# Attention units staggered: a unit's loads, scores and softmax traced ahead of its predecessor's outputs

## The chip, the cores and the metric

The kernel runs on 1 core of one Trainium2 chip. The metric is the device time of an execution in microseconds (us). "PE" is TensorE (matmuls), "ACT" ScalarE, "DVE" VectorE, "POOL" GpSimd, "SP" the engine that issues nearly all transfers.

## The reference, cut to what matters

```
scores = q @ k^T / sqrt(D)             # q, k, v: (4, 8, 576, 64), float32
scores = where(0 <= i - j < 128, scores - slope[h] * |i - j|, -1e9)
attn   = softmax(scores)
x      = (attn @ v) as (2304, 512)     # tokens x (head, d)
h      = relu(x @ w_in1);  g = s * h * h + b;  y = g @ w_out1
out    = relu(y @ w_in2) ** 2 @ w_out2 # d_model 512, d_ff 2048 in both layers
```

The attention is windowed: a query sees itself and the 127 keys before it. Two feed-forward layers follow. All is float32; the weights come as 64-bit words.

## The kernel before, in words

The 2304 tokens are cut into nine blocks of 256: eight blocks (b, u), batch b and half u of the first 512 positions, and one "tail" block of the last 64 positions of all batches. `blocks` lists them in that order, so block 0 is (0, 0), block 1 (0, 1), block 2 (1, 0), block 3 (1, 1).

Attention of a block is done head pair by head pair, four pairs (HP = 4). `pair_unit` (L190) gives two closures for a pair. `probabilities` (L200) issues the loads of the pair's q, k and v into one buffer `raw`, splits q and k into a high and a low float32r part (`qk`, an ACT copy and a DVE subtraction, L231), makes the scores on PE (L237, tile `s`), adds the bias and takes the row maximum on DVE (L178), exponentiates on ACT (L182) and inverts the denominators on DVE (L185, L186). `outputs` (L247) scales the probabilities (L260 on DVE, L258 on ACT), transposes them on PE (L262, tile `t`, named `tp` in the code), copies them out (ACT, L97), multiplies them with v (L273, tile `u`), and splits the result into the block's inputs `x(b, u)h` (ACT, L94) and `x(b, u)l` (DVE, L100). Units below are written p0 to p3 and o0 to o3: `probabilities` and `outputs` of a block's pairs 0 to 3.

Buffers of the units: `raw` comes from a ring of three (`qkv`), held from the load until the v multiplication; the probabilities come from a ring of four (`pr`), two to a unit, which also holds the rows that go out at the end of a feed-forward block (`result`, tile `xo`); the score banks are two (`s`), `t` and `u` have one bank each, the outputs of a feed-forward block two (`o`), its hidden activations two (`h`).

`mlp` (L326) runs the first layer on a block: for every 128 columns f of d_ff, `first` makes h with twelve matmuls (L348) and squares and splits it (ACT and DVE, L357, L358, L97, L100, tile `g`), and two f later `second_t` adds its product with w_out to the bank (twelve matmuls, L384). The list `behind` holds pieces of other work: before each f some of them are traced, spread evenly. Groups of weights are loaded (`load`, L138, with SP transfers queued behind the last `raw` load traced so far) and turned from 64-bit words to a high and a low part (`conv`, L151, ACT, DVE and POOL, L117 to L122). Weight group g has four f. The parts of groups 0 to 3 are l0/c0 to l3/c3; the last four loads of l3 are staged in the `qkv` ring too.

The sequence at the start: block 0's attention with c0; `half(0)` (block 0 with the first half of d_ff) with l1, c1 and block 1's attention behind it; `half(1)` with block 2's attention (a2) and l2; `half(2)` with c2 and the first two pieces of block 3 (a3); `other(0)` (second half of d_ff) with l3, c3 and the next three pieces of a3; then the rest, four or more pieces to a block. After the first layer the second one runs without attention.

The order of instructions on each engine is not the traced one. A scheduler runs a timeline of the program beforehand and gives each engine, at each moment, the ready instruction that was traced first. The order that comes out is fixed on the chip: an engine waits at its next instruction, whatever stands behind it.

Of the kernel before, what the change touches and what calls it, by code (L numbers as in the profile page):

```python
# [19 lines left out]
def attention_mlp2_kernel(ctx, tc, first0, first1, qkv0, qkv1, qkvt, w_in1, w_out1, s_in, b_in, w_in2, w_out2, out):  # L20
# [8 lines left out]
    B, H = qkv0.shape[:2]  # L29
    NT, DM = out.shape  # L30
    HP = H // 2
# [96 lines left out]
    def group_loads(g, wts, w_in, w_out, staging, steps):  # L128

        f0 = g * GF * P
        parts = [(w, k, n, st) for k, w, st in ((0, w_in, steps[0]), (2, w_out, steps[1])) for n in range(0, GF, st)]
        places = {}

        def load(i):  # L138
            if i == 0:
                wts.append({})  # L140
            w, k, n, step = parts[i]
            rows, n = slice(f0 + n * P, f0 + (n + step) * P), step
            if k == 0:
                w, rows, n = w[:, 2 * rows.start:2 * rows.stop], slice(None), NCC
            src = w[rows].rearrange("(a p) n -> p a n", p=P)
            t = places[i] = staging(i, f"st{g}{i}").rearrange("p a n -> p (a n)").rearrange("p (a n) -> p a n", a=n)

            with tc.issue_after(last_load[0]) if last_load else nullcontext():
                wdma.append(nc.sync.dma_start(t, src).ins)

        def conv(i):  # L151
            _, k, n, step = parts[i]
            if k not in wts[g]:
                for j in (k, k + 1):
                    wts[g][j] = wp.tile([P, GF, DM], F32R, tag=f"{GTAGS[j]}{g}", name=f"{GTAGS[j]}{g}")
            hi, lo = wts[g][k], wts[g][k + 1]
            part = (slice(None), slice(n, n + step)) if k else (slice(None), slice(None), slice(n * P, (n + step) * P))
            convert(places.pop(i).rearrange("p a (n w) -> p a n w", w=2), hi[part], lo[part])
        return [[lambda f=f, i=i: f(i) for i in range(len(parts))] for f in (load, conv)]
# [6 lines left out]
    def new_x(i):  # L166
        xt[i] = [xp.tile([P, NCC, BLK], F32R, tag="x" + y, name=f"x{i}{y}") for y in "hl"]
# [113 lines left out]
    def first_pair(u, hp):  # L281
        for p in pair_unit(0, u, hp):
            p()
# [117 lines left out]
    def finish1(nm, dram):  # L401
        def f(po):
            for t in range(2):
                xo = result(f"xo{nm}{t}")
                act_copy(xo, po[t])
                nc.sync.dma_start(dram[:, 2 * t:2 * t + 2, :].rearrange("p a n -> p (a n)"), xo)
        return f
# [16 lines left out]
    blocks = [(b, u) for b in range(B) for u in range(2)] + ["tail"]  # L424
# [6 lines left out]
    def psum(tag, name):  # L431
        return pools["ps"].tile([P, DM], F32, tag=tag, name=name)

    def attn(i):
        new_x(blocks[i])
        return [p for hp in range(HP) for p in pair_unit(*blocks[i], hp)]

    def zipped(*lists):

        lists, pieces = [(list(x), n) for x, n in lists], []  # L440
        while any(x for x, _ in lists):
            for x, n in lists:
                pieces += x[:n]
                del x[:n]
        return pieces
# [5 lines left out]
    def half(i, behind, span=1):  # L451
        mlp([(f"a{i}", xs[i], finish1(f"a{i}", half_dram[i]))], wts1, second_t, FS[:HF], behind, span)
# [19 lines left out]
    run(a0[:2] + l0[:1])  # L472
    run(zipped((a0[2:], 1), (c0, 1), (l0[1:], 1)))
    new_x(blocks[1])
    a1 = [lambda hp=hp: first_pair(1, hp) for hp in range(H // 2)]
    xs = [xt[blocks[0]], xt[blocks[1]]]
    half(0, zipped((l1, 1), (c1, 1), (a1, 2)))
    a2 = attn(2)
    half(1, zipped((a2, 3), (l2, 1)))
    xs.append(xt[blocks[2]])  # L480
    a3 = attn(3)
    half(2, zipped((c2, 2), (a3[:2], 1)))
    other(0, zipped((l3, 2), (c3, 2), (a3[2:5], 1)), 0.6)
    pending = a3[5:] + attn(4)
    for i in range(1, NHALF):
        other(i, pending[:4])
# [45 lines left out]
    def load_y(i):  # L532
        return load_x(f"b{i}", [acc_dram[i]] + half_dram[i:i + 1])
# [3 lines left out]
    i = LAST - 1  # L537
    pieces = [sum_column, lambda: ys.update({0: load_y(0)})]
# [9 lines left out]
    pieces = [zipped(*[(x, 1) for x in group_loads(g, wts2, w_in2, w_out2, in_bp, (1, 1))]) for g in range(NG)]  # L548
# [52 lines left out]
```

## Time and profile before

| what | value |
|---|---|
| time, median of 3 runs | 1015.83 us (1012.82 to 1015.87) |
| the profiled execution | 1014.96 us, span 1013.2 us |
| PE busy | 982.1 us, 97% of the span |
| DVE / ACT / POOL busy | 543.1 / 511.9 / 130.7 us |
| mean granted TensorE clock | 0.985 |

The profile counts PE as busy while any matmul is in flight. The granted clock has two levels here, 1.0 (2.4 GHz) and 0.5 (1.2 GHz). The page cuts the span in 40 slices of 25.3 us; the first-layer blocks with attention run until about 500 us, the second layer takes most of the rest.

### The profile page before, as it was taken

To read this page: it belongs to the slowest core of one execution; us is meant where nothing else is said; L and a number is where in the kernel's file an instruction comes from. 1 tells how busy PE (TensorE), PEld (TensorE's weight loads), DVE (VectorE), ACT (ScalarE), POOL (GpSimd) and SP (SyncE) were. 2 spreads that over 40 slices of the span, in tenths; PEclk is the share of its full clock that TensorE was granted. 3 is DMA by queue.
4 is the path that set the end of the run, shared out by engine and by line. 5 is a ranking of instruction groups with operands and counts; after the bars stand their busy time and mean duration, and the time that the engine had idled before them with its cause. 6 is when DMAs were issued, how large, how long until landed. Compare 5 with 4: busy or idle time off the path is not lost.

```text
span 1013.2 us, 18690 instructions
## 1 busy us (share of the span) xinstructions
PE 982.1 (97%) x7272; PEld 895.1 (88%) x7272; DVE 543.1 (54%) x1378; ACT 511.9 (51%) x1285; POOL 130.7 (13%) x118
## 2 busy tenths in 40 slices
PE   7799889999999999999999989999999999999998
PEld 4588778999989999899999989899998999999897
DVE  6997988343564545644276778844333333333232
ACT  7977766454464445654256677644232322323232
POOL 4653645000000000000011233200000000000000
PEclk9799989999999999999999989999999999999999
DMA  8135423111221212210043454312010000000000
GB/s 332 42 134 176 149 84 105 52 54 34 57 63 46 72 28 64 66 56 25 31 148 125 126 184 148 119 41 84 1 43 1 21 22 1 21 1 22 1 21 21
DMA packets 44488, 71.46 MB, mean 71 GB/s; under 512 B 4336, under 2 KB 24816, under 8 KB 44400
## 3 DMA queue, kind: packets, MB, share of 16 engines
q1 hardware_dynamic: 44400, 70.27, 21.4%
q8 instruction: 57, 0.93, 0.4%
q14 instruction: 31, 0.25, 0.1%
HBM read 59.25 MB, written 11.01 MB: 69 GB/s over the span
## 4 chain that ended last, share of the span: by engine, by line
PE 75%; DMA 8%; DVE 7%; ACT 7%; issue 3%; POOL 1%; SPq 0%; ACTq 0%; DVEq 0%; POOLq 0%
PE ob L393 17%; PE hb L348 17%; PE ha L348 13%; PE oa L384 12%; DMA st<-w_out 4%; DMA st<-w_in 3%; PE oc L384 3%; PE hc L348 3%; PE u L273 2%; PE s L237 2%; PE t L262 2%; ACT st L117 2%; DVE st L118 1%; DVE wil L100 1%; DVE ga L100 1%
## 5 line engine op out<-in xcount | busy, mean ns | idle before, releaser
L393 PE MATMUL ob<-woh,gb 128*128 128x512 f32 x576 | 198.5, 392 | 0.6 <-DVE gb L100 0.6
L384 PE MATMUL oa<-ga,woh 128*128 128x256 f32 x960 | 187.9, 289 | 6.2 <-DVE ga L100 3.4
L384 PEld LDWEIGHTS oa<-ga,woh 128*128 128x128 f32 x960 | 153.0, 194 | 10.2 <-DVE ga L100 4.7
L384 PE MATMUL oa<-ga,wol 128*128 128x256 f32 x480 | 137.2, 288 | 0.0
L358 DVE SCALAR_TENSOR_TENSOR rb<-hb,rb 128x256 f32<-128x256 f32 x144 | 61.0, 423 | 128.9 <-ACT rb L357 126.2
L393 PEld LDWEIGHTS ob<-woh,gb 128*128 128x128 f32 x576 | 108.6, 189 | 20.8 <-DVE gb L100 1.0
L357 ACT ACTIVATE rb<-hb 128x256 f32<-128x256 f32 x144 | 55.1, 383 | 137.5 <-PE hb L348 133.6
L393 PE MATMUL ob<-wol,gb 128*128 128x512 f32 x288 | 113.5, 394 | 0.0
L121 POOL TENSOR_TENSOR st<-st 128x512 int32<-128x512 int32 (+1 forms) x50 | 70.7, 1413 | 217.3 <-DVE st L120 154.7
L100 DVE TENSOR_TENSOR gb<-rb,gb 128x256 fp32r<-128x256 f32 x144 | 64.9, 452 | 58.4 <-ACT gb L97 36.5
L384 PEld LDWEIGHTS oa<-ga,wol 128*128 128x128 f32 x480 | 93.0, 194 | 0.5 <-DVE wol L100 0.2
L97 ACT ACTIVATE gb<-rb 128x256 fp32r<-128x256 f32 x144 | 60.1, 418 | 65.3 <-DVE rb L358 65.2
L100 DVE TENSOR_TENSOR ga<-ra,ga 128x256 fp32r<-128x256 f32 x120 | 64.5, 541 | 26.3 <-ACT ga L97 26.0
L358 DVE SCALAR_TENSOR_TENSOR ra<-ha,ra 128x256 f32<-128x256 f32 x120 | 50.1, 419 | 48.3 <-ACT ra L357 47.9
L97 ACT ACTIVATE ga<-ra 128x256 fp32r<-128x256 f32 x120 | 49.3, 413 | 40.0 <-DVE ra L358 39.2
L357 ACT ACTIVATE ra<-ha 128x256 f32<-128x256 f32 x120 | 45.1, 378 | 40.7 <-PE ha L348 38.1
L118 DVE SCALAR_TENSOR_TENSOR st<-st 128x512 int32<-128x512 int32 (+1 forms) x50 | 48.7, 977 | 24.3 <-ACT st L117 23.5
L393 PEld LDWEIGHTS ob<-wol,gb 128*128 128x128 f32 x288 | 54.6, 189 | 6.8
L117 ACT ACTIVATE st<-st 128x512 int32<-128x512 uint32 (+1 forms) x50 | 40.5, 813 | 27.5 <-DMA st<-w_out 14.1
L182 ACT ACTIVATE pr<-pr,nd 128x256 f32<-128x256 f32 (+1 forms) x96 | 45.1, 473 | 4.3 <-DVE nd L178 4.2
L119 ACT ACTIVATE st<-st 128x512 f32<-128x512 f32 (+1 forms) x50 | 40.7, 817 | 10.0 <-DVE st L118 10.0
L178 DVE CUSTOM_DVE_ANT_0 pr<-s,bases 128x256 f32<-128x256 f32 (+1 forms) x96 | 32.1, 386 | 21.5 <-PE t L262 14.7
(262 smaller groups left out, 2593.6 us busy)
## 6 DMA issues: line engine op xcount, KB each, us to landing
st<-w_out SPq DMA_DIRECT2D x20, 512.0 KB, 3.6
st<-w_in SPq DMA_DIRECT2D x8, 1024.0 KB, 5.8
st<-w_in SPq DMA_DIRECT2D x16, 512.0 KB, 4.2
st<-w_out SPq DMA_DIRECT2D x6, 1024.0 KB, 9.4
raw<-qkv SPq DMA_DIRECT2D x36, 128.0 KB, 2.7
xib<-acc SPq DMA_DIRECT2D x9, 512.0 KB, 3.9
out<-obb SPq DMA_DIRECT2D x16, 256.0 KB, 2.2
raw<-qkv SPq DMA_DIRECT2D x24, 160.0 KB, 3.0
```

Source lines behind the costliest of these rows:

```text
L97: return nc.scalar.activation(o, i, AF.Copy)
L100: nc.vector.tensor_tensor(o, a, b_, ALU.subtract)
L117: nc.scalar.activation(l32, l32.bitcast(U32), AF.Copy, scale=2.0 ** -29)
L118: nc.vector.scalar_tensor_tensor(l32, h32, -2 ** 31, l32, ALU.bitwise_and, ALU.bitwise_or)
L119: nc.scalar.activation(h32.bitcast(F32), h32.bitcast(F32), AF.Copy, scale=2.0 ** -112)
L121: nc.gpsimd.tensor_tensor(l32, h32, l32, ALU.add)
L182: nc.scalar.activation(pr, pr, AF.Exp, bias=nmx, scale=-1.0, accum_out=den)
L348: nc.tensor.matmul(ph, w_[:, cc, j * P:(j + 1) * P], x_[:, cc, :], start=(k == 0), stop=(k == 3 * NCC - 1))
L357: nc.scalar.activation(r, ph, AF.Relu)
L358: nc.vector.scalar_tensor_tensor(r, ph, 0.0, r, ALU.max, ALU.mult)
L384: nc.tensor.matmul(po[o // 2][:, (o % 2) * BLK:(o % 2 + 1) * BLK], w_[:, j, o * P:(o + 1) * P], g[:, gi, :], start=(start and n == 0 and o ...
L393: nc.tensor.matmul(po[t], g[:, gi, t * P:(t + 1) * P], w_[:, j, :], start=(start and n == 0), stop=(stop and n == 2))
```

## The change

The units of a block are traced in another order: `p0 p1 o0 p2 o1 p3 o2 o3` in place of `p0 o0 p1 o1 p2 o2 p3 o3`. Block 0 keeps the old order. Block 1's list has eight pieces in place of four (a piece was a whole pair), and four of them are taken to a turn in place of two. Nothing is added to or taken from the computation, and no buffer changes. Since the lists `behind` are cut by count, a cut now falls elsewhere: `half(2)` has p0 and p1 of block 3 behind it (before: p0 and o0), `other(0)` has o0, p2, o1 (before: p1, o1, p2).

```diff
+    def staggered(units):
+
+        pieces = [units[0][0]]
+        for a, b in zip(units, units[1:]):
+            pieces += [b[0], a[1]]
+        return pieces + [units[-1][1]]
+
     def attn(i):
         new_x(blocks[i])
-        return [p for hp in range(HP) for p in pair_unit(*blocks[i], hp)]
+        return staggered([pair_unit(*blocks[i], hp) for hp in range(HP)])
...
     new_x(blocks[1])
-    a1 = [lambda hp=hp: first_pair(1, hp) for hp in range(H // 2)]
+    a1 = staggered([pair_unit(0, 1, hp) for hp in range(HP)])
     xs = [xt[blocks[0]], xt[blocks[1]]]
-    half(0, zipped((l1, 1), (c1, 1), (a1, 2)))
+    half(0, zipped((l1, 1), (c1, 1), (a1, 4)))
```

## Rows read from the trace of the kernel before

**Rows 1.** The page: the span, and PE's busy share and clock in 40 slices.
```profile
span 1013.2 us, 18690 instructions
...
PE   7799889999999999999999989999999999999998
...
PEclk9799989999999999999999989999999999999999
```

**Rows 2.** Windows: stretch, each engine's busy us (instructions), clock, DMA share, GB/s.
```profile
110.00:135.00 25.00, 17.76 (x124) 13.61 (x123) 23.55 (x39) 17.07 (x38) 17.46 (x10) 0.87 0.46 147
121.70:125.20 3.50, 3.50 (x18) 2.95 (x17) 2.93 (x10) 2.46 (x5) 3.34 (x3) 0.51 0.85 319
132.00:138.80 6.80, 6.50 (x32) 5.86 (x33) 6.75 (x10) 4.17 (x8) 2.02 (x2) 0.50 0.01 2
...
185.00:250.00 65.00, 65.00 (x556) 60.17 (x555) 26.89 (x97) 31.91 (x89) 0.00 (x0) 1.00 0.13 40
```

**Rows 3.** Timeline of PE, 107 to 137 us: start, duration, instruction, [idle before, releaser].
```profile
111.87 0.44 PE L273 MATMUL u<-pt,raw 128*64 128x128 f32 x4 [1.13 <-DVE x(1, 0)l L100]
...
113.84 0.38 PE L384 MATMUL oa<-ga,woh 128*128 128x256 f32 x1 [0.86 <-DVE ga L100]
...
121.49 0.39 PE L384 MATMUL oa<-ga,woh 128*128 128x256 f32 x1 [2.19 <-DVE ga L100]
...
129.63 0.41 PE L262 MATMUL t<-ident,pr 128*128 128x128 f32 x2 [1.17 <-DVE pr L260]
130.88 0.44 PE L262 MATMUL t<-ident,pr 128*128 128x128 f32 x2 [0.84 <-DVE pr L260]
132.31 1.09 PE L262 MATMUL t<-ident,pr 128*128 128x128 f32 x4 [0.99 <-DVE pr L260]
```

**Rows 4.** Timeline of DVE, 119 to 134 us.
```profile
119.33 2.11 DVE L100 TENSOR_TENSOR ga<-ra,ga 128x256 fp32r<-128x256 f32 x1
...
128.25 4.17 DVE L260 TENSOR_SCALAR pr<-pr,nd 128x256 f32<-128x256 f32 x4
132.34 1.21 DVE L118 SCALAR_TENSOR_TENSOR st<-st 128x1024 int32<-128x1024 int32 x1
133.48 0.74 DVE L358 SCALAR_TENSOR_TENSOR ra<-ha,ra 128x256 f32<-128x256 f32 x2
```

**Rows 5.** Timeline of the SP queue (transfers issued), 60 to 175 us.
```profile
95.18 1.11 SPq L173 DMA_DIRECT2D raw<-qkv  x2
...
116.23 1.11 SPq L173 DMA_DIRECT2D raw<-qkv  x2
...
143.49 11.47 SPq L149 DMA_DIRECT2D st<-w_out  x3
...
164.03 1.12 SPq L173 DMA_DIRECT2D raw<-qkv  x2
```

**Rows 6.** Timeline of ACT, 106 to 166 us.
```profile
120.98 0.74 ACT L97 ACTIVATE qk<-raw 128x640 fp32r<-128x640 f32 x1 [3.07 <-DMA raw<-qkv]
121.62 0.58 ACT L97 ACTIVATE pt<-t 128x512 f32<-128x512 f32 x1
...
161.35 1.09 ACT L97 ACTIVATE xoa<-oa 128x512 f32<-128x512 f32 x2
...
164.35 0.69 ACT L97 ACTIVATE woh<-st 128x512 fp32r<-128x512 f32 x1
```

**Rows 7.** Timeline of PE, ahead of x(0, 1)'s last chunk, and the end of `other(0)`.
```profile
81.68 0.28 PE L384 MATMUL oa<-ga,wol 128*128 128x256 f32 x1
...
188.12 0.40 PE L384 MATMUL oc<-gc,woh 128*128 128x256 f32 x2
```

**Rows 8.** Timeline of PE, 84 to 96 us: block 2's units.
```profile
84.16 1.23 PE L237 MATMUL s<-qk 64*128 64x128 f32 x12
86.84 0.27 PE L262 MATMUL t<-ident,pr 128*128 128x128 f32 x1
...
94.48 0.66 PE L273 MATMUL u<-pt,raw 128*64 128x128 f32 x8
```

**Rows 9.** Timeline of POOL, 119 to 134 us, then 161 to 169 us.
```profile
129.41 1.26 POOL L493 TENSOR_TENSOR csum<-csum,woh 128x512 f32<-128x512 f32 x1
...
164.15 1.34 POOL L493 TENSOR_TENSOR csum<-csum,wol 128x512 f32<-128x512 f32 x1 [0.69 <-DVE wol L100]
```

## The prediction

> **What bounds the kernel now.** I read the slices first: PE is below nine tenths in the first two, in the fifth and sixth (101 to 152 us) and in the last; its clock is below 9 in the second, in the sixth and once near 590 us, where no attention is left [rows 1]. The windows then show two regimes. From 185 us on PE is busy for 65.00 of 65 us with DVE at 26.89 and ACT at 31.91 [rows 2]: attention lies wholly beside matmuls, and 556 matmuls in 65 us make 0.117 us each. There an order of units can win only what it costs PE to go from one kind of matmul to another. From 110 to 135 us it is the other way round: DVE is busy for 23.55 of 25 us, PE for 17.76, at a clock of 0.87 [rows 2]. That is where `half(1)` hands over to `half(2)`, which needs the last chunk of x(1, 0), while DVE converts weight group 2. So the timeline of PE is read there: six waits, 1.13 + 0.86 + 2.19 = 4.18 us on the last unit of block 2 and on `g`, and 1.17 + 0.84 + 0.99 = 3.00 us for the scaled probabilities of block 3's first pair [rows 3]. Behind both the clock was at half, for 3.5 and 6.8 us [rows 2], which is 1.7 and 3.4 us of work lost. All of it is 7.2 + 5.1 = 12.3 us, and it is nearly all that this change can win; block 0's own order, before 50 us, is left alone.
>
> **The change part by part.** No instruction is added or removed. Only trace order changes, that is, who goes first when two are ready. The profiled execution took 1014.96 us, 1.8 more than its span and 0.87 less than the median shown; the sum starts from it.
>
> *o0 of block 3 leaves `half(2)`.* Behind `half(2)` stand now p0 and p1, and o0 follows in `other(0)`. The three transposes that waited 3.00 us were o0's: PE stood at them while the first matmuls of `half(2)` had all their inputs. DVE in the same 4.17 us did only o0's four scalings, and the two squarings (L358) that feed `half(2)` came behind them at 133.48 [rows 4]. With o0 traced after all of `half(2)`, both go first. I take the 3.00 us and the 3.4 us of the half clock after it as gone: -6.4. Bounds: 0, if the scheduler still finds a gap for o0 there, and -6.4. What is late next there is `g` through DVE, which has 2 us of slack in 25.
>
> *The last unit of block 2.* p3 is traced one f earlier, o3 at the same f. But p3's `raw` load left at 95.18 [rows 5], when o0 of that block gave back its buffer of the ring of three, and o0 is now one f later. In the same queue ACT waited 3.07 us for the `raw` of block 3's p1, with o3's copy (`pt`, 0.58) behind it [rows 6]; that wait is on the path of the 2.19 and may go or grow. I take 0, between -5.9 (4.18 + 1.7, all of it) and +3.1 (that wait once more).
>
> *Loads.* The first load of l2's second half is now queued behind p3's `raw` in place of p2's, so it leaves at about 96 us rather than 84; its group is first used by `other(0)`, after 160 us: 0. Of l3 more is at stake. Three w_out loads left between 143.49 and 154.96 us [rows 5], the first when o0 gave back its `raw`, the others when converted parts did. With o0 in `other(0)` that buffer comes free some 20 us later, and p2's `raw`, which left at 164.03 [rows 5], now stands in SP's queue ahead of the last two. The last part took 11.4 us from its issue to its last subtraction (154.6 to 166.0; its ACT copy is the one at 164.35 [rows 6]). Step by step: third last part issued at 151 and done at 162; p2's `raw`; the next at 163 to 165, done at 176; the last at 174 to 176, done at 185 to 187. PE wants it for the last twelve matmuls of `other(0)`, which ended at 188.5 [rows 7], so from 187 on. That is no slack at all: 0 if it holds, +6 if it comes 4 us late and a half clock follows. I take +1, near the lower end, since the next block's `first` can fill about 3 x 1.4 us (3 x 12 matmuls).
>
> *The rows out of `half(2)`.* They need two of four `pr` buffers, and p0 and p1 now hold all four until o0's transposes are done. Their copies stood at 161.35 [rows 6]; the bank they empty is the one that `other(0)` adds into. o0 takes four scalings (0.35 each undisturbed), two rounds of transposes of 0.6 and one copy of 0.58 between them, about 3.2 us, some of it beside three `first` of `other(0)`. I take +2, between 0 and +4.2 (with a second copy and a wait).
>
> *Block 1.* Its last outputs are traced one f of `half(0)` later (sixth, before: fifth), a step of 24 matmuls, 2.8 us; its probabilities come earlier. PE had `oa` matmuls left until 81.68 [rows 7] and the last chunk of x(0, 1) came just then. 0, between -2 and +4.5.
>
> *All later blocks.* 0, between -1 and +1, with the cover named above.
>
> Sum: -6.4 + 1 + 2 = -3.4, so 1014.96 - 3.4 = 1011.6.
>
> **The rivals.** *The order is so already* (no change). While o0 of block 2 was under way, twelve score matmuls of the next pair ran at 84.16, before o0's transposes at 86.84 and its outputs at 94.48 [rows 8]: the scheduler itself had put p1 first. Against it stand the cuts of the lists, which move o0 of block 3 by a whole block. Time 1014.96, give or take 1.5.
>
> *The wait moves along with o0* (no change). The scalings took 1.04 us each while POOL summed w_out rows in 1.26 us each [rows 4, 9], and a `ga` subtraction took 2.11. POOL sums again between 162 and 169 us [rows 9], where o0 goes. Then the 3.00 us are paid there, and with the two costs above it is 1014.96 - 6.4 + 3 + 3 = 1014.6. The Trainium skill ("SBUF — State Buffer", section "SBUF: two separate sides") says that a VectorE operation in a two-port mode, or with two SBUF inputs, and a GpSimd operation exclude each other for a whole instruction. The trace agrees in kind (a scaling waits about one POOL instruction); by that rule it depends on who starts first, which no trace order sets.
>
> *Buffers* (slower). Two units in flight hold all of `pr` and two thirds of the `qkv` ring at each cut, so `xo` and the last parts of l3 wait at once: the +4.2 and the +6 above. It decides if the last w_out part is ready after 188 us. With o0's gain halved, 1014.96 - 3.2 + 4.2 + 4 = 1020. For it: three loads spread over 11.47 us already [rows 5]. Against: PE never waited for w_out there. The Trainium skill ("Perfetto Trace Analysis", section "Optimization Strategy") reads the same gap repeating on the engine that should be saturated as a sign that tiles cannot be allocated. No such gap stands in the trace before, from 185 us on PE has none; by that rule one would appear at each hand-over.
>
> *Block 1 late* (slower). A step of 2.8 us idle before `half(1)` and 1.7 us for a half clock behind it: 1014.96 + 4.5 = 1019.5 if nothing is won.
>
> **How the numbers follow.** Forecast 0.46, order already so 0.14, wait moves along 0.10, buffers 0.18, block 1 late 0.12. A measurement of this kernel tells about 0.3% (3 us) from no change. Of the forecast's 0.46, 0.42 lie beyond 3 us below the median (under 1012.8), where I put 1004 to 1012.8, and 0.04 in the band; of the two quiet rivals 0.22 in the band and 0.02 above. Faster 0.42, same 0.26, slower 0.02 + 0.18 + 0.12 = 0.32. The range goes from 1004 (-6.4 and most of the -5.9) to 1021 (buffers and a little); the forecast's own range is 1004 to 1014.
>
> **What would show it.** Right: no transposes of block 3 between 125 and 155 us, no half clock there, scores of its p1 before 155. The ring: w_out loads leaving past 160 us, PE waiting for `wol` or `gc` between 180 and 195. The `pr` ring: `xo` copies of `half(2)` after o0's transposes. Block 1: PE idle ahead of x(0, 1). I am wrong if transposes still stand in `half(2)`, or if DVE delays `g` as much without o0.

## The result, and the profile after

The kernel after takes 1020.52 us (median of 7 runs, 1018.63 to 1021.43), the kernel before beside it 1014.71 us (7 runs, 1012.82 to 1016.19). The ratio is 1.0051, 95% interval 1.0036 to 1.0065: slower by 5.2 us by the ratio (3.7 to 6.6), 5.8 between the medians, where 1011.6 was forecast. The profiled execution is the one of 1020.52 us.

The page of after (against [rows 1]): the span, and PE's busy share and clock in 40 slices.
```profile
span 1018.7 us, 18675 instructions
...
PE   6799979999999999999999989999999999999998
...
PEclk9798979999999999999999999999999999999999
```
PE's clock falls in the fourth slice (76 to 102 us), which was full before, and still in the sixth.

Windows of before (one row that did not stand above) and then of after: stretch, busy us (instructions) of PE, PEld, DVE, ACT, POOL, clock, DMA share, GB/s.
```profile
85.00:95.00 10.00, 10.00 (x85) 8.72 (x83) 7.58 (x35) 7.08 (x25) 0.00 (x0) 1.00 0.38 120
```
```profile
85.00:95.00 10.00, 7.84 (x48) 6.37 (x46) 7.09 (x33) 5.49 (x19) 0.23 (x1) 0.66 0.12 30
110.00:135.00 25.00, 19.33 (x155) 15.94 (x153) 23.47 (x40) 19.33 (x43) 15.37 (x10) 0.95 0.40 131
...
130.00:135.00 5.00, 1.95 (x8) 1.03 (x8) 4.93 (x7) 2.23 (x4) 4.69 (x5) 0.76 1.04 405
135.00:140.00 5.00, 3.38 (x16) 2.29 (x17) 5.00 (x14) 3.26 (x9) 2.47 (x2) 0.50 0.25 97
185.00:250.00 65.00, 65.00 (x539) 60.04 (x538) 27.86 (x98) 30.30 (x86) 0.00 (x0) 1.00 0.12 36
```
Three things differ. Between 85 and 95 us, in `half(1)`, PE starts 48 matmuls where it started 85. From 130 to 140 us, in `half(2)`, it is busy for 5.33 of 10 us with DVE at 9.93. And from 185 to 250 us it is as full as before (65.00 of 65) but starts 539 matmuls instead of 556 [rows 2].

Timeline of PE after, `half(1)` and then `half(2)` (start, duration, instruction, [idle before, releaser]).
```profile
84.33 1.23 PE L237 MATMUL s<-qk 64*128 64x128 f32 x12
...
88.02 0.33 PE L237 MATMUL s<-qk 64*128 64x128 f32 x2 [1.18 <-ACT qk L97]
89.33 1.12 PE L262 MATMUL t<-ident,pr 128*128 128x128 f32 x4 [0.98 <-ACT pt L97]
...
132.45 0.53 PE L262 MATMUL t<-ident,pr 128*128 128x128 f32 x2 [1.64 <-DVE pr L260]
133.71 0.69 PE L262 MATMUL t<-ident,pr 128*128 128x128 f32 x2 [0.73 <-DVE pr L260]
135.15 0.66 PE L262 MATMUL t<-ident,pr 128*128 128x128 f32 x2 [0.75 <-ACT pt L97]
136.40 0.69 PE L262 MATMUL t<-ident,pr 128*128 128x128 f32 x2 [0.59 <-DVE pr L260]
...
139.02 0.58 PE L348 MATMUL ha<-x(1, 0)h,wih 128*128 128x256 f32 x1 [0.88 <-DVE ra L358]
```
Timeline of ACT after, and the same line of ACT before.
```profile
87.34 0.63 ACT L97 ACTIVATE qk<-raw 128x512 fp32r<-128x512 f32 x1 [1.05 <-DMA raw<-qkv]
...
88.36 0.64 ACT L357 ACTIVATE ra<-ha 128x256 f32<-128x256 f32 x2
```
```profile
84.25 0.63 ACT L357 ACTIVATE ra<-ha 128x256 f32<-128x256 f32 x2
```
In `half(1)` ACT's queue now has the exponentials of p1 and the split of p2's `qk` ahead of the `relu` of the first two f, which comes at 88.36 and not at 84.25; ACT itself stood 1.05 us there for p2's `raw`. Until then both banks of `first` (the pool has two) are taken, so PE has only attention to do, and waits for ACT twice. From the first wait on its clock is at half, 88.2 to 95.1 us. In `half(2)` the transposes of block 3's first unit, which the forecast had sent to `other(0)`, stand where they stood [rows 3], and wait 3.71 us instead of 3.00, 0.75 of it for ACT. The eight transposes of its second unit, in `other(0)` before, stand in `half(2)` now as well (147.3 to 151.2 us). A half clock comes again (132.6 to 142.9).

Timelines of DVE, of the SP queue and of ACT after (against [rows 4], [rows 5], [rows 6]).
```profile
127.38 2.31 DVE L100 TENSOR_TENSOR wol<-st,woh 128x1024 fp32r<-128x1024 f32 x1
...
131.09 5.25 DVE L260 TENSOR_SCALAR pr<-pr,nd 128x256 f32<-128x256 f32 x4
```
```profile
144.47 0.33 SPq L149 DMA_DIRECT2D st<-w_out  x1
158.60 1.11 SPq L173 DMA_DIRECT2D raw<-qkv  x2
...
160.53 0.33 SPq L149 DMA_DIRECT2D st<-w_out  x1
...
168.70 0.33 SPq L149 DMA_DIRECT2D st<-w_out  x1
```
```profile
166.79 1.07 ACT L97 ACTIVATE xoa<-oa 128x512 f32<-128x512 f32 x2
```
The four scalings take 5.25 us (before 4.17). The last loads of l3 and the rows out of `half(2)` come later, as foreseen.

To place the loss in all kernels I took, at five moments of each trace, the time less the nominal length of the matmuls started so far (each kind at its mean start-to-start time behind 185 us), and from that the same for the kernel before. It counts idle time, half clock and breaks between kinds of matmuls alike. For after it is +5.6 us at 95 us, +4.1 at 145, +2.2 at 190, +4.1 at 400, +5.8 at 1000: the loss of `half(1)` is partly won back at the hand-overs, and 2.6 us more go between 190 and 490 us, where PE waits for 0.4 us in all.

How much of it is chance can be read where the order of the instructions on PE, DVE and ACT is that of before. only_a2 has that order until 85 us and stands at +1.8 there; late_alone has it until 215 us and stands at -1.1 at 190. Behind 490 us all kernels have the same order, and the measure still moves by -0.9 to +2.9 us up to 700. So differences under 2 us between two traces tell little by themselves, and what goes behind 490 us can't be put down to the order of the units.

### The profile page after: what moved, and what is told of

It is laid out like the page before. It is cut to its first block, busy times and chain, and to the rows that moved or that the text cites. A ratio compares the mean times of both kernels' runs of the same rounds, so it can differ in the third digit from the quotient of the medians.

```text
span 1018.7 us, 18675 instructions
## 1 busy us (share of the span) xinstructions
PE 983.6 (97%) x7272; PEld 895.6 (88%) x7272; DVE 543.5 (53%) x1378; ACT 509.1 (50%) x1285; POOL 131.4 (13%) x118
## 4 chain that ended last, share of the span: by engine, by line
PE 78%; DVE 8%; DMA 7%; ACT 4%; issue 2%; SPq 0%; DVEq 0%; ACTq 0%
PE ob L393 17%; PE hb L348 17%; PE ha L348 15%; PE oa L384 14%; DMA st<-w_in 4%; PE oc L384 4%; PE hc L348 3%; PE s L237 3%; PE u L273 2%; PE t L262 2%; DMA st<-w_out 2%; DVE st L118 2%; ACT st L117 1%; DVE ga L100 1%; DVE wol L100 1%
## 5 line engine op out<-in xcount | busy, mean ns | idle before, releaser
L384 PE MATMUL oa<-ga,wol 128*128 128x256 f32 x480 | 136.2, 286 | 0.3 <-DVE wol L100 0.3
L121 POOL TENSOR_TENSOR st<-st 128x512 int32<-128x512 int32 (+1 forms) x50 | 70.5, 1410 | 230.5 <-DVE st L120 174.8
L100 DVE TENSOR_TENSOR ga<-ra,ga 128x256 fp32r<-128x256 f32 x120 | 61.1, 512 | 29.3 <-ACT ga L97 28.6
```

Of the source, the lines that this page charges most:

```text
L100: nc.vector.tensor_tensor(o, a, b_, ALU.subtract)
L121: nc.gpsimd.tensor_tensor(l32, h32, l32, ALU.add)
L384: nc.tensor.matmul(po[o // 2][:, (o % 2) * BLK:(o % 2 + 1) * BLK], w_[:, j, o * P:(o + 1) * P], g[:, gi, :], start=(start and n == 0 and o ...
```

## The experiments

15 kernels, in four groups, each run beside the kernel before (medians 1014.85, 1015.34, 1015.22 and 1015.33 us). "Lost" is the measure just told, against before, from one profiled execution each.

| kernel | median us | ratio to before, 95% | lost at 95, 145, 190, 400, 1000 us |
|---|---|---|---|
| after | 1020.52 | 1.0036-1.0065 | +5.6, +4.1, +2.2, +4.1, +5.8 |
| cut_alone | 1024.67 | 1.0084-1.0119 | +5.5, +6.5, +8.8, +8.5, +7.9 |
| a1_alone | 1021.80 | 1.0048-1.0077 | +2.7, +3.3, +4.7, +4.6, +5.1 |
| late_old | 1021.11 | 1.0037-1.0073 | +4.3, +3.2, +1.6, +2.1, +3.6 |
| a1_cut_as_before | 1018.58 | 1.0017-1.0048 | -0.1, -1.1, -0.9, +0.5, +4.5 |
| late_alone | 1016.47 | 1.0008-1.0028 | +0.3, -1.2, -1.1, -0.9, +2.1 |
| only_a3 | 1016.04 | 0.9995-1.0013 | 0.0, +0.1, 0.0, +0.1, +2.4 |
| only_a2 | 1019.61 | 1.0032-1.0056 | +1.6, +3.1, +5.3, +5.1, +4.8 |
| first_three | 1014.62 | 0.9989-1.0006 | +0.3, -1.1, -0.7, -0.6, -1.2 |
| a1_earlier | 1024.21 | 1.0069-1.0106 | +1.7, +5.4, +5.1, +7.5, +9.3 |
| before_sums_late | 1014.80 | 0.9984-1.0011 | -0.7, -3.6, -4.5, +0.6, +1.0 |
| after_sums_late | 1016.46 | 0.9999-1.0021 | +0.1, -3.3, -5.4, +1.4, +2.7 |
| first_three_sums_late | 1017.99 | 1.0010-1.0036 | -0.9, -4.3, -4.3, +2.3, +2.9 |
| before_sums_end | 1011.88 | 0.9950-0.9975 | -1.0, -4.3, -5.0, -8.5, -3.1 |
| after_sums_end | 1014.89 | 0.9980-1.0004 | +1.2, -2.4, -4.5, -3.4, +1.0 |
| first_three_sums_end | 1011.36 | 0.9942-0.9966 | -0.6, -4.6, -4.6, -7.5, -4.9 |

### Which part of the change costs

*cut_alone*: nothing staggered; block 1's list in eight pieces, four to a turn.
```
-    a1 = staggered([pair_unit(0, 1, hp) for hp in range(HP)])
+    a1 = [p for hp in range(HP) for p in pair_unit(0, 1, hp)]
```


> No stagger at all: block 1's units in the old order, but as eight pieces taken four to a turn, as the changed kernel cuts them. Theory 'cut' (the finer cut traces block 1's last outputs one f of half(0) later, and the first relu of half(1) is then queued behind the softmax of block 2's second pair; 4.7 us by the traces): 1018 to 1020 us, with a half-clock stretch near 88 to 95 us. Theory 'stagger' (two units in flight cost time wherever they are): 1014.7, as before.

*a1_cut_as_before*: everything staggered; block 1's list in four pieces of two, two to a turn.
```
+    a1 = [lambda p=p: run(p) for p in (a1[0:2], a1[2:4], a1[4:6], a1[6:8])]
...
-    half(0, zipped((l1, 1), (c1, 1), (a1, 4)))
+    half(0, zipped((l1, 1), (c1, 1), (a1, 2)))
```


> All blocks staggered, but block 1's eight pieces are fused to four, so that every cut of half(0) stands where it stood before the change. Theory 'cut': the 4.7 us come back, 1015 to 1016 us, and the relu of half(1) stands ahead of block 2's p1 again. Theory 'stagger': 1020, no change. In either, if the transposes of block 3's first pair now spread over half(2), the wait of 3 to 4 us and the half clock there go too and it may be 1011 to 1013.

*a1_alone* and *late_old*: only block 1 staggered; only blocks 1 to 3.
```
-        return staggered([pair_unit(*blocks[i], hp) for hp in range(HP)])
+        units = [pair_unit(*blocks[i], hp) for hp in range(HP)]
+        return staggered(units) if i in [2, 3] else [p for u in units for p in u]
```
(with `[]` for a1_alone)

> Only block 1 staggered, cut in eight as in the change; blocks 2 to 7 in the old order. Theory 'cut': 4.7 us of the 5.8 are here, 1018.5 to 1020. Theory 'stagger': block 1 is one of seven blocks, so 1015 to 1016. Theory 'later blocks' (3.3 us lost after 180 us by scores cut into finer groups among the matmuls): about 1017, since the 3.3 are missing here.

> Blocks 1 to 3 staggered as in the change, blocks 4 to 7 in the old order. Theory 'later blocks': 3.3 us less than the changed kernel, about 1017. Theory 'cut' alone: 1020, no difference from the changed kernel, and the same loss curve after 180 us.

The cut alone, without any stagger, loses 9.8 us, 5.5 of them by 95 us; with four pieces of block 1 that loss is gone. Windows of cut_alone around the start of `half(1)`:
```profile
75.00:80.00 5.00, 3.87 (x28) 2.84 (x26) 5.00 (x8) 3.68 (x8) 4.76 (x4) 1.00 0.80 227
80.00:85.00 5.00, 4.73 (x41) 4.19 (x41) 5.00 (x5) 1.69 (x3) 3.61 (x4) 1.00 0.16 61
85.00:95.00 10.00, 8.45 (x74) 7.07 (x75) 7.71 (x37) 7.08 (x27) 1.13 (x1) 1.00 0.62 201
```
DVE is busy throughout while x(0, 1)'s last outputs are made, and PE short of work. So `half(1)` starves without any stagger: block 1's last outputs are piece 12 of the 16 in `half(0)`'s list and were piece 8 of 12, so x(0, 1) is ready later against block 0's matmuls. DVE ends its last chunk 0.7 us behind the last matmul of `half(0)` before, 2.1 us in after and 2.5 in cut_alone. The loss does not have one shape, though. cut_alone has lost 3.9 us by 85 us and has no half clock near 88 us, so its expectation (1018 to 1020, with that half clock) missed. after has lost 1.0 by 85 us and loses 4.5 in the ten behind it. a1_alone, with much the same two waits for ACT (1.04 and 0.50 us) and a full clock, loses 1.6 there.

The sizes missed as well. a1_cut_as_before still loses 3.7 us in the median, none of it before 190 us. a1_alone loses 7.0, more than each of its three theories had it and no less than the whole change. late_old, with the old order behind block 3, is no faster than after.

*late_alone*, *only_a3*, *only_a2*, *first_three*: the same edit with `[4, 5, 6, 7]`, `[3]` and `[2]` (block 1 as before), and with `[2, 3]` beside a staggered block 1 in four pieces.

> Only blocks 4 to 7 are staggered; blocks 1 to 3 keep the order and the cuts of before. Later-blocks theory: their finer mixing of attention and first-layer matmuls costs PE about 3 us between 185 and 500 us, without any idle row, so 1017 to 1019, and the first 180 us as before. Rival (attention that lies beside matmuls costs the same in any order, and the rise was an after-effect of the start): 1014 to 1016.

> Only block 3 is staggered. The prediction's first step (outputs of its first unit leave half(2), and 3.0 us of waits and 3.4 us of half clock go with them): 1008 to 1010. Rival, gap filling (the scheduler still puts transposes of block 3 into half(2), because it has nothing else ready there): some three to eight of them still stand in half(2) with their waits, 1013 to 1016.

> Only block 2 is staggered. The prediction took 0 for its last unit, between -5.9 and +3.1. Cut theory (the loss in half(1) comes from the cut of block 1's list alone): no half clock between 80 and 100 us, 1013 to 1017. Rival (the staggered block 2 takes gaps of half(1) and is a part of the loss there): PE idle and a half clock near 88 us, 1018 to 1020.

> Blocks 1 to 3 staggered, block 1 traced in the four pieces of before, blocks 4 to 7 in the order of before. If the terms add (no starved half(1), no finer mixing behind 185 us): 2 to 3 us under the kernel with block 1's cut alone taken back, so 1014 to 1016, perhaps 1 us under the kernel before. Rival (the rest of that kernel's loss is not in the later blocks but in the start of the second layer): 1017 to 1019.

Timelines of PE in `half(2)`: only_a3, only_a2, then first_three.
```profile
133.35 1.09 PE L262 MATMUL t<-ident,pr 128*128 128x128 f32 x4 [4.55 <-DVE pr L260]
```
```profile
133.31 0.41 PE L262 MATMUL t<-ident,pr 128*128 128x128 f32 x2 [3.27 <-DVE pr L260]
...
137.10 0.58 PE L348 MATMUL ha<-x(1, 0)h,wih 128*128 128x256 f32 x1 [1.85 <-DVE ra L358]
...
169.70 0.39 PE L384 MATMUL oc<-gc,woh 128*128 128x256 f32 x1 [2.22 <-DVE gc L100]
```
```profile
125.60 2.25 PE L237 MATMUL s<-qk 64*128 64x256 f32 x12 [2.66 <-DVE nd L178]
131.78 0.58 PE L348 MATMUL ha<-x(1, 0)h,wih 128*128 128x256 f32 x1 [2.78 <-DVE ra L358]
...
136.17 0.38 PE L262 MATMUL t<-ident,pr 128*128 128x128 f32 x2
...
152.66 0.38 PE L262 MATMUL t<-ident,pr 128*128 128x128 f32 x2
...
155.52 0.28 PE L348 MATMUL hc<-x(0, 0)h,wih 128*128 128x256 f32 x1
```
Timeline of DVE in first_three.
```profile
122.22 2.29 DVE L100 TENSOR_TENSOR wol<-st,woh 128x1024 fp32r<-128x1024 f32 x1
...
126.15 2.22 DVE L100 TENSOR_TENSOR wol<-st,woh 128x1024 fp32r<-128x1024 f32 x1
...
131.31 0.74 DVE L358 SCALAR_TENSOR_TENSOR ra<-ha,ra 128x256 f32<-128x256 f32 x2
```
These rows decide the forecast's first step. only_a3 keeps the transposes in `half(2)`; they wait once, for 4.55 us. In first_three they go behind the first two squarings (136.2 to 158.5 us, six of the eight still ahead of `other(0)`, whose first matmul is the one at 155.52) and wait for nothing. Nothing is won by it: PE waits 2.66 us for the maxima of the scores and 2.78 us for the squarings, and the clock is at half for 10.2 us (124.8 to 135.0) where it was for 6.8. In no run do all eight leave `half(2)`, as the forecast wanted. DVE is the late engine whichever of its products comes next. only_a2 missed its expectation of 1013 to 1017: `half(1)` loses nothing (the 1.6 us are lost ahead of it, where the order is still that of before) and has no half clock, yet the hand-overs cost 3.7 us more, with DVE as releaser each time.

first_three against a1_cut_as_before changes the order of blocks 4 to 7 alone: the ratios differ by 0.0035, 3.5 us. The same blocks changed by themselves, in late_alone, cost 1 to 3 us; changed back in the kernel after, in late_old, they gain nothing (1021.11 us against 1020.52). Windows of first_three, then of a1_cut_as_before:
```profile
190.00:400.00 210.00, 210.00 (x1798) 192.13 (x1797) 103.87 (x394) 109.19 (x333) 1.81 (x12) 1.00 0.17 51
```
```profile
190.00:400.00 210.00, 209.61 (x1782) 191.59 (x1781) 103.01 (x391) 107.24 (x328) 1.83 (x12) 1.00 0.17 50
```
Both are full, one with 16 matmuls fewer (16 x 0.117 = 1.9 us). From the starts of all matmuls there: in a1_cut_as_before 25 groups of scores begin behind a matmul of the layer, in first_three 18. The step into such a group takes 0.21 us and the step out of one 0.24, against 0.07 between two scores and 0.13 between two matmuls of the layer. One group more thus costs some 0.25 us (an estimate: 0.21 + 0.24 - 0.07 - 0.13), seven of them 1.8. The measure bears that out: between 190 and 490 us the kernels that stagger blocks 4 to 7 lose 1.1 to 3.7 us (late_alone, a1_cut_as_before, after, a1_earlier), the others with POOL's sums in their old place -0.1 to +0.7. Another 3 us of a1_cut_as_before go between 600 and 700 us, where no attention is left; late_alone and only_a3 show 2 us there too. Two waits for `rb` of 1.2 to 1.5 us stand in that stretch. The order is the same there in all kernels, so this is not shown to be the change's; why the waits come in some traces is open.

### Is it the place of block 1's outputs?

*a1_earlier*: the kernel after with all eight pieces taken at once, so that the last is piece 10 of 16.
```
-    half(0, zipped((l1, 1), (c1, 1), (a1, 4)))
+    half(0, zipped((l1, 1), (c1, 1), (a1, 8)))
```


> The kernel after, all blocks staggered and block 1 still in eight pieces, but all eight taken at once: its last outputs are piece 10 of 16 in half(0) (after: 12 of 16; before: 8 of 12). Position theory (half(1) starves because x(0, 1)'s last chunk comes late against block 0's matmuls, not because there are more pieces): no half clock near 88 us, 2 to 4 us under the kernel after, so 1016.5 to 1018.5. Rival (eight fine pieces starve it wherever they stand): the half clock near 88 us stays, 1020 to 1022.

Windows of a1_earlier:
```profile
85.00:95.00 10.00, 10.00 (x87) 9.26 (x86) 6.90 (x29) 7.00 (x27) 1.63 (x2) 1.00 0.15 57
120.00:145.00 25.00, 15.52 (x98) 12.78 (x94) 24.96 (x47) 17.14 (x39) 16.77 (x10) 0.66 0.46 147
```
The place theory is right about `half(1)`: 87 matmuls, full clock. It is wrong about the time, 1024.21 us, the second worst of all. What `half(1)` no longer loses is lost at the hand-over, with DVE busy for 24.96 of 25 us and POOL for 16.77, and 4 us more go behind 190 us.

### What makes DVE late

POOL spends 48.6 us between 37 and 169 us (25.2 + 23.4, 16 sums of each kind) on 32 sums of weight rows (`csum`), for a column needed only by the second layer. An estimate from the traces: between 37 and 170 us DVE's instructions take 33.5 us longer than the same forms take undisturbed (the lower quartile of their lengths in all traces), 18.9 us of it beside a sum and 14.6 beside one of POOL's adds for the weight conversion (L121). In the next kernels csum starts from an activation chunk times zero in place of a memset, so that the sums can't start before that chunk is there. *..._sums_late* (behind x(2, 0), in the kernel before, the kernel after and first_three):
```
-    nc.gpsimd.memset(csum, 0.0)
+    nc.gpsimd.tensor_scalar(csum, xt[blocks[4]][0][:, :2, :].rearrange("p c n -> p (c n)").bitcast(F32), 0.0, None, ALU.mult)
```


> The kernel before, with the 32 row sums of POOL held back: csum starts from x(2, 0) times zero (in place of a memset), so that they run from about 220 us on, where DVE has slack. The order of half(1) and half(2) is that of before. DVE-and-POOL theory (the stage before 160 us is bound by DVE, and its instructions are stretched by POOL's sums): a `pr` scaling below 0.6 us in place of 1.1, a `ga` subtraction near 0.5 in place of 1.36, PE waits at the hand-over cut by half or more, 1007 to 1012. Rival (the hand-over waits for a chain of PE, ACT and loads, DVE only stands at its end): 1013.5 to 1016.

> The kernel after with the same 32 row sums held back. If the loss to the kernel before comes only from the starved half(1) and the later blocks, it stays 3 to 6 us above the kernel before with late sums: 1011 to 1017. Rival (what the stagger lost was DVE time against POOL): it comes within 2 us of the kernel before with late sums.

> Blocks 1 to 3 staggered, block 1 in four pieces, blocks 4 to 7 as before, and the 32 row sums held back. In this kernel no transposes of block 3 wait in half(2), and the waits for squarings and maxima on DVE took their place. If DVE is what they wait for, shorter DVE instructions free them: 1005 to 1010, and below the kernel before with late sums by 1 to 3 us. Rival (the order of units is worth nothing there even with DVE free): the same as the kernel before with late sums, within 1 us.

By 190 us all three are 4.3 to 5.4 us ahead of the kernel before, and after_sums_late lies level with before_sums_late (-5.4 and -4.5). But the sums ran from 235 to 290 us, and there the gain went back. The window of before_sums_late, where the kernel before is full:
```profile
250.00:255.00 5.00, 4.42 (x38) 3.91 (x37) 4.50 (x7) 2.38 (x8) 4.78 (x5) 1.00 0.16 41
```
So the medians of before_sums_late (in its rival's range) and first_three_sums_late (above both of its ranges) missed their expectations, though the start did what the theory said; after_sums_late is 1.7 us above before_sums_late, as its rival had it. *..._sums_end* puts them behind x(3, 1), from about 430 us:
```
-    nc.gpsimd.memset(csum, 0.0)
+    def start_sums():
+        xh = xt[blocks[LAST - 1]][0][:, :2, :].rearrange("p c n -> p (c n)").bitcast(F32)
+        nc.gpsimd.tensor_scalar(csum, xh, 0.0, None, ALU.mult)
...
+        late = [start_sums] + sums if i == LAST - 2 else []
...
-        mlp(..., zipped((pending + more[:5], 2), (sums[:4], 1)))
+        mlp(..., zipped((pending + more[:5], 2), (late, 1)))
```


> The kernel before with the 32 row sums behind x(3, 1)'s first two chunks (csum starts from them times zero), so that they run from about 430 us on. DVE-and-POOL theory: the 4.6 us won before 200 us stay, since DVE has most slack there: 1009.5 to 1012. Rival (the sums cost as much wherever they run): 1013.5 to 1016.

> The kernel after with the sums behind x(3, 1). DVE-and-POOL theory: the start loses no more than in the kernel before with sums at the end, what is left are the later blocks' 1 to 3 us: 1010.5 to 1014, that is 0 to 3 us above it. Rival (the order of units costs 5 us by itself): 1014.5 to 1018, 4 us or more above it.

> Blocks 1 to 3 staggered, block 1 in four pieces, blocks 4 to 7 as before, sums behind x(3, 1). DVE-and-POOL theory: neither the starved half(1) nor the later blocks' share, so within 1.5 us of the kernel before with sums at the end: 1009 to 1012. Rival: 1013 to 1017.

Windows and the timeline of DVE of before_sums_end, whose traced order in `half(1)` and `half(2)` is that of before (the order that the scheduler makes of it differs from 48 us on):
```profile
110.00:135.00 25.00, 19.56 (x136) 16.15 (x135) 20.98 (x43) 18.53 (x39) 8.45 (x4) 0.80 0.46 147
...
425.00:500.00 75.00, 71.47 (x599) 67.43 (x596) 35.88 (x90) 28.82 (x82) 44.43 (x37) 0.98 0.10 31
```
```profile
125.47 1.14 DVE L260 TENSOR_SCALAR pr<-pr,nd 128x256 f32<-128x256 f32 x4
```
Four scalings take 1.14 us where they took 4.17 [rows 4]; DVE is busy for 20.98 us in place of 23.55, PE for 19.56 in place of 17.76 [rows 2]. PE no longer waits for `pr` there, and between 37 and 170 us DVE's instructions take 12.7 us longer than undisturbed in place of 33.5, all of it beside the weight conversion. A half clock stays (124.0 to 134.2 us). The kernel before gains 3.5 us in all, though the sums still cost PE 3.5 us of idle time at the end. Behind 190 us its trace order differs too, since the sums no longer sit in the lists with the attention pieces: of the 8.5 us won by 400 us, at most the 5.0 before 190 are those of DVE and POOL, and what the scheduler's other order did to them is not shown apart.

With the sums at the end in both, the kernel after is 3.0 us behind the kernel before, and no longer 5.8. What is left is almost all in blocks 4 to 7: after_sums_end and first_three_sums_end are level at 190 us (-4.5, -4.6) and 4.1 us apart at 400. Windows of first_three_sums_end, then of after_sums_end:
```profile
190.00:400.00 210.00, 210.00 (x1825) 194.03 (x1824) 104.83 (x398) 110.35 (x335) 1.81 (x12) 1.00 0.18 54
```
```profile
190.00:400.00 210.00, 209.92 (x1786) 191.98 (x1785) 101.62 (x384) 106.27 (x326) 1.82 (x12) 1.00 0.17 50
```
39 matmuls fewer at the same busy time: 39 x 0.117 = 4.6 us. Groups of scores begin behind the layer's matmuls 25 times against 15, which is 2.5 us at 0.25 us each; the rest is open. first_three_sums_end, 1011.36 us, is 0.34 to 0.58% under the kernel before and the fastest here; against before_sums_end the stagger of blocks 1 to 3 is worth nothing that can be told.

## Why the prediction was wrong, point by point

*What bounds the kernel.* The place was right (the first 160 us, the hand-over, DVE at 23.55 of 25 us) and the conclusion was not. The forecast treated the wait of the transposes as theirs: move them, and 6.4 us go. It said itself that DVE was nearly full, and then gave `g` "2 us of slack in 25" (25 less 23.55 is 1.45). Its reading of the slices also left one out: PE stands at eight tenths in the 24th (583 to 608 us) too.

*"o0 of block 3 leaves `half(2)`", -6.4.* This is the step that failed, twice over. The transposes did not leave, so the bound that stood beside it (0, "if the scheduler still finds a gap for o0 there") held. And they were not what PE stood at: the first matmuls of `half(2)` had their inputs, but no bank. Timeline of PE before:
```profile
128.18 0.28 PE L348 MATMUL ha<-x(1, 0)h,wil 128*128 128x256 f32 x1
...
134.37 0.58 PE L348 MATMUL ha<-x(1, 0)h,wih 128*128 128x256 f32 x1
```
With the one at 128.18 the 24 matmuls of two f were done and both banks of `first` taken; the next began when DVE had squared one, at 133.48 [rows 4]. Where the transposes went behind the squarings, in first_three, DVE had two weight subtractions of 2.2 to 2.3 us and the maxima ahead of them (131.31), and the waits for `nd` and `ra` took the place of those for `pr` (2.66 + 2.78 us, for 3.00). The step's worth can't be told from 0 either way (only_a3 0.9995 to 1.0013, first_three 0.9989 to 1.0006).

*"The last unit of block 2", 0, bounds -5.9 to +3.1.* Staggering block 2 alone costs 4.3 us (3.2 to 5.7), outside the range; 3.7 us of the profiled execution's loss arise at both hand-overs behind it.

*"Loads", +1, and the rows out of `half(2)`, +2.* Both came later, as worked out (w_out loads at 160.5 and 168.7, the `xoa` copies at 166.79 in place of 161.35), and cost nothing to be seen: PE waits 0.4 us in all between 145 and 200 us, and the loss falls from 4.1 to 2.2 us between 145 and 190. With it the rival *buffers* falls.

*"Block 1", 0, bounds -2 to +4.5.* The shift by one f was seen, its price mis-sized: +4.5 us between 85 and 95 us in after, and 5 to 8 us for block 1 alone (a1_alone), beyond the bound. The rival *block 1 late* (1019.5) is the nearest to what happened, with a half clock where it put one; but PE lost the time inside `half(1)`, behind ACT, and not ahead of it.

*"All later blocks", 0, between -1 and +1.* Mis-sized, and by how much is not settled: 3.5 us in two pairs of medians (first_three against a1_cut_as_before, and the pair with sums at the end), 1 to 3 in late_alone, nothing in late_old against after; 1.1 to 3.7 us in the traces by 490 us. That PE was busy for 65 of 65 us was read as cover; it hides waits, but not the breaks between kinds of matmuls, which are counted as busy.

*The wait moves along.* This rival, at 0.10, named the cause, DVE slowed by POOL's sums, though not the path: o0 stayed, and nothing was paid in `other(0)`. Putting the sums off gave the kernel before 3.5 us, where the change gave nothing. The terms of the change do not add, either: block 1 alone +7.0, block 2 alone +4.3, block 3 alone +0.7, blocks 4 to 7 alone +1.1, blocks 1 to 3 together, with block 1 in four pieces, -0.7 (block 3's and the last can't be told from 0). While DVE is full, each order only chooses which product is late.

*The order is so already.* On PE this rival, at 0.14, was right for block 2 and for the first pairs of block 3: before, p2 of block 2 was through at 92.5 us and o1 began at 95.1, and p1 of block 3 stood at 126.0 with o0 at 129.6. The stagger had little left to move there; the cuts of the lists and block 1 are what it did move.

## What to carry to other kernels

Where an engine off the bound is busy for nine tenths of a stretch, a wait on it is not the waiting instruction's: moving that instruction renames the wait, and the engine's own work has to shrink first. Look beside a slow VectorE instruction for what GpSimd does in the same microseconds, and put off what has no reader yet. An order that mixes attention more finely with other matmuls costs TensorE time even where it never waits (some 0.25 us a group here): count the matmuls started in a full stretch, not its busy share.

## What the runs showed of the hardware

Only some DVE instructions are stretched by POOL. Groups of DVE before, 115 to 140 us (count, busy us, mean ns of one), then of before_sums_end:
```profile
L100 DVE TENSOR_TENSOR ga<-ra,ga 128x256 fp32r<-128x256 f32 x3 | 4.5, 1507 | 0.0
L260 DVE TENSOR_SCALAR pr<-pr,nd 128x256 f32<-128x256 f32 x4 | 4.2, 1100 | 0.0
...
L358 DVE SCALAR_TENSOR_TENSOR ra<-ha,ra 128x256 f32<-128x256 f32 x5 | 2.0, 414 | 0.2 <-ACT ra L357 0.2
```
```profile
L100 DVE TENSOR_TENSOR ga<-ra,ga 128x256 fp32r<-128x256 f32 x5 | 3.7, 756 | 0.0
...
L358 DVE SCALAR_TENSOR_TENSOR ra<-ha,ra 128x256 f32<-128x256 f32 x5 | 2.1, 418 | 0.5 <-ACT ra L357 0.5
```
The squaring, which reads `ha` from a PSUM bank, takes 0.41 us in both. The mean of the `ga` subtraction mixes two lengths, and who started first decides: 0.42 us at 130.28 in before_sums_end, where POOL began an add at 130.44, and 2.12 at 138.97, where POOL had begun one at 138.80. These adds belong to the weight conversion and stay when the sums are put off; the long `ga` subtractions before stood beside them, too (119.33 and 135.87 us). What the sums lengthened here are the scalings. The Trainium skill ("SBUF — State Buffer", section "SBUF: two separate sides") names the two-port modes and instructions with two SBUF inputs as those that exclude GpSimd. The trace agrees: the squaring has one SBUF input and is not slowed (0.42 us at 116.49, beside a sum from 116.25 to 117.71). The scaling has one SBUF tensor as well and is slowed; whether it runs in a two-port mode no run shows.

Two waits of PE, of 1.18 and 0.98 us and 1.3 us apart, stood at the start of 6.9 us of half clock (after, 88 us). Of the 4.5 us lost between 85 and 95 us the two make 2.2; the other 2.3 go with the half clock. In a1_alone the two were 1.04 and 0.50 us, the clock stayed full, and 1.6 us were lost.
